# Experts 1 to 7: gathered rows transposed by DMA from two 16-bit planes, joined by ScalarE

## Chip, cores, metric

One core of a Trainium2 chip. The metric is the device time of one execution in microseconds (us). Engines are named as in the profile: PE is TensorE's matmul, PEld its weight load, DVE VectorE, ACT ScalarE, POOL GpSimd and SP SyncE, which here only issues DMAs. L12 is line 12 of the kernel before, unless said otherwise.

## The reference, cut to what matters

Three stages in float32: attention with a block-causal mask, a dense layer, and a mixture of eight experts of which each token takes two. N = 2304 tokens, D = 512, E = 8 experts, hidden size F = 1024.

```python
attn = softmax(mask(q @ k.T / sqrt(64)))           # 4 batches x 8 heads x 576 x 64
x = heads_joined(attn @ v)                          # 2304 x 512
h = maximum(maximum(x @ w1, x @ w2), x @ w3)        # 512 -> 768
x = h @ w_out                                       # 768 -> 512
logits = x @ w_gate + log1p(exp(x @ w_noise)) * noise
top2 = argpartition(-logits, 2, axis=1)[:, :2]
top2_w = softmax over the two logits
for e in range(8):
    for k in range(2):
        mask = top2[:, k] == e
        out[mask] += top2_w[mask, k, None] * (maximum(x[mask] @ W1[e], 0) @ W2[e])
```

## The kernel before, in words

Every float32 product is made as three PE products of halves: a value is split into `hi` (rounded to the matmul's type) and `lo = value - hi`, and hi·hi, lo·hi and hi·lo are summed in PSUM.

**Attention and the dense layer** run interleaved up to about 500 us. The dense layer works in nine units of 256 tokens. Its output for 128 tokens, `x2` (128 x 512 float32, a tile named "x2" of the pool `keep` with two buffers), goes to the DRAM array `x2d` through `store` (L847), one DMA of 256 KB on SP. The same two "x2" buffers are used by `init_out`, which fills the output with zeros. `route` then takes the two best experts of each token and writes token number and weight into lists by expert (`ids`, DRAM).

**The experts** come in eight rounds e, the one with most tokens after expert 0 first. The rows of one expert are taken in five chunks of 128, with capacities `CAPS[e]` of 640, 640, 624, 608, 600, 592, 584 and 576 rows.
- `gather(e)` (L1146): five indirect DMAs on POOL bring the rows by their numbers `ig` from `x2d` into tiles "xg", one token in a partition.
- `transposes(e)` (L1154): four PE transposes a chunk (L1167) bring the 512 columns into partitions, in PSUM; ACT copies the result to `xh` (L1169), and DVE subtracts to `xl` (L1170). There is one buffer each of `xh` and `xl`, so expert e + 1 can only write them when the first product of expert e has read them.
- `mm1(e, f)` (L1172): for eight column groups f, the first product: rows 0 to `CAPS[e]` - 256 and the last 256 apart, 12 products each (L1179 to L1181), then ReLU and its halves on ACT and DVE (L1183, L1184).
- `mm2(e, c)` (L1210): for a chunk c of rows, 24 products (L1227 to L1229) into 512 columns. For e > 0 the earlier output rows are gathered (`prev`, L1217, on POOL), DVE multiplies by the token's weight and adds, and an indirect DMA on POOL scatters the rows to the output (L1235).
- Weights (`load_expert`, L163): six pieces an expert, 768 KB (128 x 1536) or 512 KB (128 x 1024). Each is loaded on SP (L173, L178) into one of two buffers "rw", copied to the high half by ACT (L186) and subtracted to the low half by POOL (L187). A piece is fetched by `next(nw)` in the loop over the first product's f and in the second product.

Expert 0 begins while the last unit of the dense layer runs; its hidden values take the tiles of the dense layer and others as these come free. For this `free` (L1191) holds a list of names. Its last five entries are "hx", "x2", "hx", "x2", "hx": the tail parts of the hidden values for f = 4 and f = 6, rows 384 on, lie in the two "x2" buffers. They are read by the last two chunks of expert 0's second product.

The main loop at the kernel's end (printed below) sets the order: for expert e the first product with the next weights between, then `gather(e + 1)`, then the second product, with `transposes(e + 1)` behind its third chunk (behind the fourth chunk for e = 0). The program is scheduled by the framework from that order: each engine has its own instructions in a fixed order and waits on semaphores.

Of the kernel before, what the change touches and what calls it, by code (L numbers as in the profile page):

```python
# [7 lines left out]
F32 = mybir.dt.float32  # L8
# [4 lines left out]
U16 = mybir.dt.uint16  # L13
AF = mybir.ActivationFunctionType
# [3 lines left out]
B, H, S, D = 4, 8, 576, 64  # L18
DM, FF = 512, 768
NTOK = B * S  # L20
E, F2, CAP = 8, 1024, 640
# [4 lines left out]
CAPS = (640, 640, 624, 608, 600, 592, 584, 576)  # L26
# [3 lines left out]
CE = 3  # L30
# [94 lines left out]
def plain(ap):  # L125
    return ap.bitcast(F32)
# [3 lines left out]
def tile_attention_moe_moe(ctx, tc, qT, kT, v, w1, w2, w3, w_out, gates, noise, e1, e2, out):  # L130
    nc = tc.nc
# [3 lines left out]

    w1, w2, w3, w_out = (x.bitcast(I32) for x in (w1, w2, w3, w_out))
    x2d = nc.dram_tensor("x2d", [NTOK, DM], F32).ap()
    xld = nc.dram_tensor("xld", [4, 128, 2, UT], F32).ap()
    owd = nc.dram_tensor("owd", [E * NTOK, 1], F32).ap()
    ids = nc.dram_tensor("ids", [E * CAP, 2], F32).ap()  # L140
# [20 lines left out]
    XG, XGT = {}, {}  # L161
# [30 lines left out]
    keep = ph3.enter_context(tc.tile_pool(name="keep", bufs=1))  # L192
    moe = ph2.enter_context(tc.tile_pool(name="moe", bufs=1))
    att = ph1.enter_context(tc.tile_pool(name="att", bufs=1, side="right"))
# [17 lines left out]
    def new_set(q, kv, p, pt):  # L212
        nc.gpsimd.memset(p[:, 448:704].rearrange("p (a c) -> p a c", a=2)[:, :, 0:64], 0.0)
        SET.append((q, kv[:, 0:256], kv[:, 256:512].rearrange("p (r c) -> p r c", r=2), p,
                    pt.rearrange("p (r c) -> p r c", r=2)))

    new_set(*(att.tile([128, n], F32, name=x) for x, n in (("qe", 512), ("kve", 512), ("pe", 768), ("pte", 768))))
    LT = {x: n for x, n in (("Qh", 640), ("Ql", 640), ("Kh", S), ("Kl", S), ("V", 1280), ("Ph", 2560), ("Pl", 2560))}
    t = {x: att.tile([128, n], F32, name=x) for x, n in LT.items()}
    new_set(t["Qh"][:, :512], t["Kh"][:, :512], t["Ph"][:, :768], t["Ph"][:, 768:1536])  # L220
    new_set(t["Ql"][:, :512], t["Kl"][:, :512], t["Ph"][:, 1536:2304], t["Pl"][:, :768])
    new_set(t["V"][:, :512], t["V"][:, 512:1024], t["Pl"][:, 768:1536], t["Pl"][:, 1536:2304])

    nc.vector.tensor_scalar(ident, jp, 0.0, None, op0=OP.is_equal)
    nc.vector.tensor_scalar(before, jp, 0.0, None, op0=OP.is_gt)
# [20 lines left out]
    RAW, VV, QK, ST = {}, {}, {}, {}  # L246

    def at(j):
        late, b, g = JOBS[j]
        return b * H + 2 * g  # L250
# [27 lines left out]

    def load_values(j):
        n = LJ.index(j) % 2  # L280
        VV[j] = att.tile([128, 1280 if n else 640], F32, name=("rv", "V")[n])[:, :640].rearrange("p (r c) -> p r c", r=2)
        nc.sync.dma_start(VV[j], v[at(j):at(j) + 2].rearrange("h p c d -> p h (c d)"))

    def split_keys(j, low):
# [354 lines left out]
    def start():  # L639
# [141 lines left out]
        add("SP", 1.0, lambda: nc.sync.dma_start(noise_sb, noise.rearrange("(t p) e -> p t e", p=128)), [x, q8], 5.0, late=2.0, load=5.0)  # L781
        v8 = add("SP", 0.45, lambda: load_rest(8), [EV[7]], 4.0, late=2.0, load=0.5)
        add("SP", 0.45, lambda: load_values(first), [EV[6]], 4.0, late=2.0, load=0.8)
        add("POOL", 0.45, late_tails, [], 4.0)
        late_q = [add("POOL", 0.65, lambda n=n: late_queries(n), [ES[4 + n, 0], ES[4 + n, 1]], 3.0) for n in (0, 1)]
# [61 lines left out]
    def store(u, tt, x2):  # L847
        r0 = (u * 2 + tt) * 128
        nc.sync.dma_start(x2d[r0:r0 + 128, :], x2)

    def logits():
        return keep.tile([128, 2, 2 * E], F32, name="gl", bufs=2)
# [47 lines left out]
    rows = consts.tile([128, NU * 2, 2, 2], F32, name="rows")  # L900
# [147 lines left out]
    def late_after(j):  # L1048
        return next((x for x in LJ if x > j), NJ)
# [28 lines left out]
    for tt in range(2):  # L1078
        store(0, tt, C0[tt])
# [4 lines left out]
    RAW.pop(first)  # L1084
    load_job(late_after(first))
    load_values(late_after(first))
    scored(8)
    gap(8)
    for j in range(8, NJ):
        b, g = JOBS[j][1:]  # L1090
        T, SS = turn_steps(j), score_steps(j + 1)
        for n in range(max(len(T), len(SS))):
            if n < len(T):
                T[n]()
            if n < len(SS):
                SS[n]()
            gap(j)
        if j + 1 < NJ:
            scored(j + 1)
        pv(j)  # L1100
        if LATE[j]:
            n = late_after(j)
            if n < NJ:
                n = late_after(n)
                if n < NJ:
                    load_values(n)
        elif following(j):
            load_rest(following(j))
        gap(j)
        gap(j)  # L1110
        if all(x[:2] != JOBS[j][:2] for x in JOBS[j + 1:]):
            ready.add(2 * b + LATE[j])
        if 8 <= j < 8 + NU:
            init_out(j - 8)
# [7 lines left out]
    mw = ph1.enter_context(tc.tile_pool(name="mw", bufs=1, side="right"))  # L1122
# [3 lines left out]
    def bank2():  # L1126
        turn[0] ^= 1
        if turn[0]:
            return ps2.tile([128, 512], F32, name="b")
        return psT.tile([128, 512], F32, name="t", bufs=4)  # L1130
# [14 lines left out]

    def gather(e, c0=0, c1=NCH, rows=NTOK):  # L1146
        for c in range(c0, c1):
            x = mw.tile([128, DM], F32, name="xg", bufs=6)
            nc.gpsimd.indirect_dma_start(
                out=x, out_offset=None, in_=x2d[:rows],  # L1150
                in_offset=bass.IndirectOffsetOnAxis(ap=ig[:, e, c:c + 1], axis=0))
            XG[e, c] = x

    def transposes(e, c0=0, c1=NCH):  # L1154
        if c0 == 0:
            XGT[e] = [mw.tile([128, 4, CAP], F32R, name=n) for n in ("xh", "xl")]
        th, tl = XGT[e]
        for c in range(c0, c1):
            if e == 0 and c < CE and BT:
                ps = ps2.tile([128, 512], F32, name="b")  # L1160
            else:
                ps = bank2()
            ps = ps.rearrange("p (k t) -> p k t", k=4)
            n = min(128, CAPS[e] - 128 * c)
            ps = ps[:, :, :n]
            for kt in range(4):
                nc.tensor.transpose(ps[:, kt], XG[e, c][:n, kt * 128:(kt + 1) * 128], ident[:n, :n])  # L1167
            s = slice(c * 128, c * 128 + n)
            nc.scalar.activation(th[:, :, s], ps, AF.Copy)  # L1169
            nc.vector.tensor_sub(tl[:, :, s], ps, plain(th[:, :, s]))  # L1170

    def mm1(e, f, ht, parts=None, get=bank2):  # L1172
        parts = parts or ((0, CAPS[e] - 256), (CAPS[e] - 256, CAPS[e]))
        th, tl = XGT[e]
        for c0, c1 in parts:
            ps = get()
            p = ps[:, :c1 - c0]
            for kt in range(4):
                nc.tensor.matmul(p, wt1(e, 0, kt, f), th[:, kt, c0:c1], start=kt == 0, stop=False)  # L1179
                nc.tensor.matmul(p, wt1(e, 0, kt, f), tl[:, kt, c0:c1], start=False, stop=False)  # L1180
                nc.tensor.matmul(p, wt1(e, 1, kt, f), th[:, kt, c0:c1], start=False, stop=kt == 3)  # L1181
            hi, lo = (ht(t, c0, c1) for t in range(2))
            nc.scalar.activation(hi, p, AF.Relu)  # L1183
            nc.vector.scalar_tensor_tensor(lo, p, 0.0, plain(hi), op0=OP.max, op1=OP.subtract)  # L1184

    def hidden_tile(pool):
        t = pool.tile([128, 2, CAP], F32R, name="ht", bufs=8)
        return lambda s, c0, c1: t[:, s, c0:c1]
# [5 lines left out]
    def spare(shape):  # L1194
        pool, n, c = free.pop(0)
        return pool.tile(shape, F32R, name=n, bufs=c)
# [46 lines left out]
    def weights_of(e):  # L1243
        for m in range(2):
            yield from load_expert(e, m, rw)
# [88 lines left out]
    for e in range(E):  # L1334
        nw = weights_of(e + 1) if e + 1 < E else iter(())
        if e == 1:
            ph2.close()
            hid = ph2.enter_context(tc.tile_pool(name="hid", bufs=1))
        if e:
            HT = [hidden_tile(hid) for _ in range(8)]  # L1340
        for f in range(8):
            if e:
                mm1(e, f, HT[f])
            else:
                more[f].append(spare([128, 2, CAP - 128 * CE]))
                mm1(e, f, HT[f], ((128 * CE, CAP),))
            if f in (0, 1, 3, 6):
                next(nw, None)
        if e + 1 < E:
            gather(e + 1)  # L1350
        for c in range(0 if e else CE, NCH):
            mm2(e, c, HT)
            if c == (0 if e else CE):
                next(nw, None)
            if c == (2 if e else CE) and e + 1 < E:
                transposes(e + 1)
        for _ in nw:
            pass
    ph1.close()
# [98 lines left out]
```

## Time and profile before

| | |
|---|---|
| median of 3 runs | 985.82 us (985.78 to 988.04) |
| profiled execution | 986.13 us |
| its span, first to last instruction | 984.4 us |
| mean granted clock of TensorE | 0.998 of full speed |
| PE busy | 971.0 us, 99%, 6594 instructions |
| DVE busy | 431.2 us, 44% |
| ACT busy | 395.5 us, 40% |
| POOL busy | 392.6 us, 40% |
| DMA | 106.17 MB, 108 GB/s over the span |

The times of the text are those of the profiled execution, counted from the span's start. A busy share is the time in which an engine works on instructions, over the span; DMA issues on POOL count as POOL work of about 1 us each. Matmuls overlap: one shows a duration of 0.39 us and the next starts 0.23 us after it. The spacing of two starts tells what one costs.

### The profile page before, as it was taken

To read this page: it belongs to the slowest core of one execution; us is meant where nothing else is said; L and a number is where in the kernel's file an instruction comes from. 1 tells how busy PE (TensorE), PEld (TensorE's weight loads), DVE (VectorE), ACT (ScalarE), POOL (GpSimd) and SP (SyncE) were. 2 spreads that over 40 slices of the span, in tenths; PEclk is the share of its full clock that TensorE was granted. 3 is DMA by queue.
4 is the path that set the end of the run, shared out by engine and by line. 5 is a ranking of instruction groups with operands and counts; after the bars stand their busy time and mean duration, and the time that the engine had idled before them with its cause. 6 is when DMAs were issued, how large, how long until landed. Compare 5 with 4: busy or idle time off the path is not lost. (4 is left out here: it accounts for less than half of the span.)

```text
span 984.4 us, 17147 instructions
## 1 busy us (share of the span) xinstructions
PE 971.0 (99%) x6594; PEld 861.2 (87%) x6594; DVE 431.2 (44%) x1259; ACT 395.5 (40%) x938; POOL 392.6 (40%) x298
## 2 busy tenths in 40 slices
PE   9999999999999999999999999999999999999997
PEld 5856899999898998999999889898988979898895
DVE  7854657654677665632355322222222222221321
ACT  7587545544565555531134234142323323132210
POOL 3595121211213013120221577755836556564302
PEclk9999999999999999999999999999999999999999
DMA  9912414221211312212022546543535354452101
GB/s 322 340 29 71 134 47 155 54 90 31 62 55 36 92 36 68 63 30 85 22 81 82 173 160 196 180 151 108 184 108 162 109 155 146 126 170 77 52 14 57
DMA packets 72550, 106.17 MB, mean 108 GB/s; under 512 B 19196, under 2 KB 44796, under 8 KB 72464
## 3 DMA queue, kind: packets, MB, share of 16 engines
q1 hardware_dynamic: 61120, 75.93, 24.1%
q0 software_dynamic: 10224, 28.32, 8.8%
q8 instruction: 53, 0.87, 0.4%
q10 hardware_dynamic: 1120, 0.79, 0.3%
q14 instruction: 33, 0.27, 0.1%
HBM read 85.35 MB, written 20.53 MB: 108 GB/s over the span
## 5 line engine op out<-in xcount | busy, mean ns | idle before, releaser
L187 POOL TENSOR_TENSOR w<-rw,w 128x1536 fp32r<-128x1536 f32 (+1 forms) x42 | 131.7, 3137 | 71.7 <-ACT w L186 56.2
L827 POOL TENSOR_TENSOR hl<-hm,hh 128x512 fp32r<-128x512 f32 x21 | 27.7, 1317 | 173.3 <-ACT hh L826 173.2
L186 ACT ACTIVATE w<-rw 128x1536 fp32r<-128x1536 f32 (+1 forms) x42 | 56.5, 1345 | 89.2 <-issue 42.1
L1179 PE MATMUL b<-xh,w 128*128 128x384 f32 (+7 forms) x272 | 87.4, 322 | 0.7 <-DVE xB L1184 0.4
L1180 PE MATMUL b<-xl,w 128*128 128x384 f32 (+7 forms) x272 | 87.4, 321 | 0.3 <-DVE xl L1170 0.3
L1181 PE MATMUL b<-xh,w 128*128 128x384 f32 (+7 forms) x272 | 87.6, 322 | 0.0
L811 PE MATMUL t<-xA,w 128*128 128x256 f32 x288 | 83.1, 289 | 0.0
L812 PE MATMUL t<-xA,w 128*128 128x256 f32 x288 | 81.7, 284 | 0.0
L813 PE MATMUL t<-xA,w 128*128 128x256 f32 x288 | 81.5, 283 | 0.0
L1184 DVE SCALAR_TENSOR_TENSOR ht<-b,ht 128x384 fp32r<-128x384 f32 (+6 forms) x56 | 29.1, 520 | 94.3 <-ACT ht L1183 94.3
L1235 POOL DMA_INDIRECT out_rows<-y,isc x37 | 37.5, 1013 | 77.3 <-DVE y L1232 73.1
L1180 PE MATMUL t<-xl,w 128*128 128x256 f32 x240 | 67.3, 280 | 0.0
L1181 PE MATMUL t<-xh,w 128*128 128x256 f32 x240 | 67.3, 280 | 0.0
L1179 PE MATMUL t<-xh,w 128*128 128x256 f32 x240 | 67.3, 281 | 0.0
L1227 PE MATMUL b<-w,ht 128*128 128x512 f32 (+1 forms) x168 | 67.0, 399 | 0.0
L291 POOL TENSOR_TENSOR Kl<-rk,Kh 128x576 fp32r<-128x576 f32 x16 | 23.2, 1450 | 109.0 <-ACT Kh L288 109.0
L1229 PE MATMUL b<-w,ht 128*128 128x512 f32 (+1 forms) x168 | 66.4, 395 | 0.0
L1228 PE MATMUL b<-w,ht 128*128 128x512 f32 (+1 forms) x168 | 66.3, 394 | 0.0
L999 POOL DMA_INDIRECT ids<-rows,slots x36 | 35.9, 996 | 68.4 <-DVE slots L996 60.1
L811 PE MATMUL t<-xB,w 128*128 128x256 f32 x216 | 61.9, 287 | 0.0
L812 PE MATMUL t<-xB,w 128*128 128x256 f32 x216 | 61.3, 284 | 0.0
L813 PE MATMUL t<-xB,w 128*128 128x256 f32 x216 | 61.2, 283 | 0.0
(404 smaller groups left out, 2766.7 us busy)
## 6 DMA issues: line engine op xcount, KB each, us to landing
rw<-in_e SPq DMA_DIRECT2D x32, 768.0 KB, 4.6
w<-in_w SPq DMA_DIRECT2D x18, 512.0 KB, 7.8
rw<-in_e SPq DMA_DIRECT2D x16, 512.0 KB, 3.7
rk<-in_kT SPq DMA_DIRECT2D x16, 288.0 KB, 2.8
x2d<-x SPq DMA_DIRECT2D x18, 256.0 KB, 2.0
out_rows<-x SPq DMA_DIRECT2D x9, 512.0 KB, 3.0
w<-in_w_out SPq DMA_DIRECT2D x6, 512.0 KB, 10.1
rq<-in_qT SPq DMA_DIRECT2D x16, 160.0 KB, 2.3
```

Of the source, the lines that this page charges most:

```text
L186: nc.scalar.activation(t[:, 0, :c], r[:, :c], AF.Copy)
L187: nc.gpsimd.tensor_sub(t[:, 1, :c], r[:, :c], plain(t[:, 0, :c]))
L811: nc.tensor.matmul(ps[:, j], wh, x[:, 0], start=kt == 0, stop=False)
L812: nc.tensor.matmul(ps[:, j], wh, x[:, 1], start=False, stop=False)
L813: nc.tensor.matmul(ps[:, j], wl, x[:, 0], start=False, stop=kt == 3)
L1179: nc.tensor.matmul(p, wt1(e, 0, kt, f), th[:, kt, c0:c1], start=kt == 0, stop=False)
L1180: nc.tensor.matmul(p, wt1(e, 0, kt, f), tl[:, kt, c0:c1], start=False, stop=False)
L1181: nc.tensor.matmul(p, wt1(e, 1, kt, f), th[:, kt, c0:c1], start=False, stop=kt == 3)
L1227: nc.tensor.matmul(ps, a, wt2(e, 0, f), start=f == 0, stop=False)
L1228: nc.tensor.matmul(ps, a, wt2(e, 1, f), start=False, stop=False)
L1229: nc.tensor.matmul(ps, l, wt2(e, 0, f), start=False, stop=f == 7)
L1235: st = nc.gpsimd.indirect_dma_start(out=out, out_offset=bass.IndirectOffsetOnAxis(ap=at, axis=0), in_=y, in_offset=None, bounds_check=NTOK ...
```

## The change

Beside `x2d` there is a second DRAM array `x2p` of 16-bit words, 1024 a token: first the low halves of its 512 float32 words, then the high halves. `store` has POOL copy `x2` into such planes (tile "xp", one buffer) and stores them with a second DMA on SP. To make room, attention's tile "V" falls from 1280 to 768 words, some load buffers are cut out of it in smaller pieces, and "xg" has five buffers instead of six.

For experts 1 to 7 `gather` reads `x2p`. `transposes` then transposes a chunk of 128 x 1024 16-bit words by one DMA on SP into a tile "x2" (the same name and two buffers as above), as eight blocks of 128 x 128. ACT joins the two planes back into 32-bit words in the chunk's "xg" tile, ACT copies to `xh` as before, now from SBUF, and POOL, not DVE, subtracts to `xl`. Expert 0 is left as it was. `transposes(e + 1)` stands right behind `gather(e + 1)`, ahead of the second product of expert e.

```diff
+    x2p = nc.dram_tensor("x2p", [NTOK, 2 * DM], U16).ap()
...
-    LT = {x: n for x, n in (("Qh", 640), ("Ql", 640), ("Kh", S), ("Kl", S), ("V", 1280), ("Ph", 2560), ("Pl", 2560))}
+    LT = {x: n for x, n in (("Qh", 640), ("Ql", 640), ("Kh", S), ("Kl", S), ("V", 768), ("Ph", 2560), ("Pl", 2560))}
...
     def store(u, tt, x2):
         r0 = (u * 2 + tt) * 128
         nc.sync.dma_start(x2d[r0:r0 + 128, :], x2)
+        planes = keep.tile([128, 2, DM], U16, name="xp", bufs=1)
+        nc.gpsimd.tensor_copy(planes, x2.bitcast(U16).rearrange("p (d h) -> p h d", h=2))
+        nc.sync.dma_start(x2p[r0:r0 + 128].rearrange("r (h d) -> r h d", h=2), planes)
...
     def gather(e, c0=0, c1=NCH, rows=NTOK):
         for c in range(c0, c1):
-            x = mw.tile([128, DM], F32, name="xg", bufs=6)
+            x = mw.tile([128, DM], F32, name="xg", bufs=5)
+            if e:
+                x = x.bitcast(U16)
             nc.gpsimd.indirect_dma_start(
-                out=x, out_offset=None, in_=x2d[:rows],
+                out=x, out_offset=None, in_=x2p if e else x2d[:rows],
                 in_offset=bass.IndirectOffsetOnAxis(ap=ig[:, e, c:c + 1], axis=0))
             XG[e, c] = x
...
         th, tl = XGT[e]
         for c in range(c0, c1):
+            if e:
+                n = min(128, CAPS[e] - 128 * c)
+                s = slice(c * 128, c * 128 + n)
+                tp = keep.tile([128, DM], F32, name="x2", bufs=2).bitcast(U16).rearrange("p (k t) -> p k t", k=8)
+                nc.sync.dma_start_transpose(tp, XG[e, c])
+                x = XG[e, c].bitcast(F32).rearrange("p (k t) -> p k t", k=4)
+                nc.scalar.activation(x.rearrange("p k t -> p (k t)").bitcast(U16).rearrange("p (c h) -> p h c", h=2),
+                                     tp.rearrange("p (h k) t -> p h (k t)", h=2), AF.Copy)
+                nc.scalar.activation(th[:, :, s], x[:, :, :n], AF.Copy)
+                nc.gpsimd.tensor_sub(tl[:, :, s], x[:, :, :n], plain(th[:, :, s]))
+                continue
...
         if e + 1 < E:
             gather(e + 1)
+            transposes(e + 1)
         for c in range(0 if e else CE, NCH):
             mm2(e, c, HT)
             if c == (0 if e else CE):
                 next(nw, None)
-            if c == (2 if e else CE) and e + 1 < E:
-                transposes(e + 1)
```

How the instructions stand is shown at two places, both between expert 0 and expert 1. A name in brackets says what a row waits for: DMASW is a gather or scatter of POOL, DMAHW an earlier DMA of SP, and PE, DVE, Activation and Pool that engine.

SP before, weight loads only (L178 and L173, an ISA row sets an address from the expert's number):

```order
L178 DMA rw<-in_e 128x2x512 [waits DMAHW5_49,DMAHW3_49,Pool_49]
L173 ISA
L173 DMA rw<-in_e 128x4x384 [waits DMAHW6_49,DMAHW4_49,Pool_49]
L173 ISA
L173 DMA rw<-in_e 128x4x384 [waits DMAHW7_49,DMAHW5_49,Pool_49]
```

SP in the changed kernel, at the same loads (their lines are now L179 and L174, and x_7032 and the like are "x2" tiles):

```order
L179 DMA rw<-in_e 128x2x512 [waits DMAHW7_49,DMAHW5_49,Pool_49]
L1169 DMA_TRANSPOSE x_7032<-xg 128x8x128 [waits DMASW4_49,DMAHW0_49,DVE_49,PE_49]
L1169 DMA_TRANSPOSE x_7037<-xg 128x8x128 [waits DMASW5_49,DMAHW1_49,DVE_49,PE_49]
L174 ISA
L174 DMA rw<-in_e 128x4x384 [waits DMAHW6_49,Pool_49]
L1169 DMA_TRANSPOSE x_7042<-xg 128x8x128 [waits DMAHW0_49,DMASW6_49,Activation_49]
L1169 DMA_TRANSPOSE x_7047<-xg 128x8x128 [waits DMAHW1_49,DMASW7_49,Activation_49]
L174 ISA
L174 DMA rw<-in_e 128x4x384 [waits DMAHW7_49,Pool_49]
L1169 DMA_TRANSPOSE x_7052<-xg 128x8x128 [waits DMAHW3_49,DMASW0_49,Activation_49]
```

The five transposes of expert 1 stand between its last weight load and the first two loads for expert 2; the first two wait for PE, the others for ACT.

POOL before, from the last but one weight piece of expert 1 on (L187 weights, L1149 gathers for expert 2, L1235 scatter, L1217 earlier output rows):

```order
L187 TENSOR_TENSOR w<-rw,w 128x1536 [waits DMAHW4_49,Activation_49]
L1149 DMA xg<-x2d,ig 128x512 [waits DMASW7_49,PE_49]
L1149 DMA xg<-x2d,ig 128x512 [waits DMASW0_49,PE_49]
L187 TENSOR_TENSOR w<-rw,w 128x1024 [waits DMAHW5_49,Activation_49]
L1235 DMA out_rows<-y,isc 2304x512 [waits DMASW1_49,DVE_49]
L187 TENSOR_TENSOR w<-rw,w 128x1536 [waits DMAHW6_49,PE_49,Activation_49]
L1217 DMA prev_5388<-out_rows,isc 128x512 [waits DMASW5_49,DMASW2_49,DMASW1_49]
L1217 DMA prev_5387<-out_rows,isc 128x512 [waits DMASW3_49]
```

POOL in the changed kernel, from that expert's last weight piece on (lines 188, 1155, 1252 and 1234 now; L1174 is the subtraction to `xl`):

```order
L188 TENSOR_TENSOR w<-rw,w 128x1024 [waits DMAHW7_49,Activation_49]
L1252 DMA out_rows<-y,isc 2304x512 [waits DMASW3_49,DVE_49]
L1174 TENSOR_TENSOR xl<-xg,xh 128x4x128 [waits DMASW4_49,Activation_49]
L1174 TENSOR_TENSOR xl<-xg,xh 128x4x128 [waits DMASW5_49,Activation_49]
L1155 DMA xg<-x2p,ig 128x1024 [waits DMAHW0_49,Pool_49]
L188 TENSOR_TENSOR w<-rw,w 128x1536 [waits DMAHW2_49,Activation_49]
L1155 DMA xg<-x2p,ig 128x1024 [waits DMAHW1_49,Pool_49]
L1234 DMA prev_5424<-out_rows,isc 128x512 [waits DMASW3_49,DMASW6_49,DMASW2_49,DMASW1_49]
L1234 DMA prev_5423<-out_rows,isc 128x512 [waits DMASW7_49]
L1174 TENSOR_TENSOR xl<-xg,xh 128x4x128 [waits Activation_49] x2
L188 TENSOR_TENSOR w<-rw,w 128x1536 [waits DMAHW5_49,Activation_49]
L1174 TENSOR_TENSOR xl<-xg,xh 128x4x128 [waits DMASW0_49,Activation_49]
```

The five subtractions of expert 1 now stand in POOL's queue among weight pieces, gathers and reads of earlier rows. PE's order there has eight products of expert 1 with xh, then the products with the first 384 rows of xl, 36 up to the first that reads the last 256.

## Rows read from the trace of the kernel before

**Rows 1.** The page's first part: busy us, share of the span, instructions.
```profile
PE 971.0 (99%) x6594; PEld 861.2 (87%) x6594; DVE 431.2 (44%) x1259; ACT 395.5 (40%) x938; POOL 392.6 (40%) x298
```

**Rows 2.** Waits of PE from 500 us on: total us, times, longest.
```profile
PE b L1179 <- DVE xB L1184: 0.4, 1, 0.4
```

**Rows 3.** PE on the tile "xg": count, ns min/median/max, first and last start, shapes.
```profile
L1167 PE MATMUL t<-ident,xg x88: 221/272/273, 511.3 to 912.7; 128*128 128x128 f32 x64, 112*128 112x112 f32 x4, 96*128 96x96 f32 x4, 88*128 88x88 f32 x4
...
L1167 PE MATMUL b<-ident,xg x72: 270/273/273, 510.9 to 912.2; 128*128 128x128 f32 x72
```

**Rows 4.** Timeline of PE, expert 0 to 1: start us, us, instruction, [idle before <-releaser].
```profile
573.66 0.49 PE L1167 MATMUL b<-ident,xg 128*128 128x128 f32 x3
...
575.65 0.48 PE L1227 MATMUL t<-w,hl 128*128 128x512 f32 x1
...
579.01 0.40 PE L1229 MATMUL t<-w,x 128*128 128x512 f32 x1
...
580.40 0.39 PE L1229 MATMUL t<-w,x 128*128 128x512 f32 x1
...
581.74 0.62 PE L1179 MATMUL b<-xh,w 128*128 128x384 f32 x2 [0.24 <-ACT xh L1169]
```

**Rows 5.** Timeline of PE in expert 1's second product.
```profile
627.54 0.60 PE L1167 MATMUL t<-ident,xg 128*128 128x128 f32 x4
...
629.61 0.48 PE L1227 MATMUL b<-w,ht 128*128 128x512 f32 x1
```

**Rows 6.** The page's DMA issues: count, KB each, median us to landing.
```profile
rw<-in_e SPq DMA_DIRECT2D x32, 768.0 KB, 4.6
...
rw<-in_e SPq DMA_DIRECT2D x16, 512.0 KB, 3.7
...
x2d<-x SPq DMA_DIRECT2D x18, 256.0 KB, 2.0
...
w<-in_w_out SPq DMA_DIRECT2D x6, 512.0 KB, 10.1
...
xg<-x2d,ig POOLq DMA_INDIRECT x40, 3.6
```

**Rows 7.** Timeline of SP's queue, expert 0 to 1.
```profile
581.86 0.37 SPq L178 DMA_DIRECT2D rw<-in_e  x1
```

**Rows 8.** Timeline of POOL, expert 0 to 1.
```profile
578.32 3.51 POOL L187 TENSOR_TENSOR w<-rw,w 128x1536 fp32r<-128x1536 f32 x1 [4.97 <-ACT w L186]
...
583.25 0.95 POOL L1149 DMA_INDIRECT xg<-x2d,ig  x1 [0.30 <-issue]
```

**Rows 9.** ACT, expert 0 to 1, then its groups by form from 500 us on (busy us, mean ns).
```profile
585.66 1.06 ACT L186 ACTIVATE w<-rw 128x1024 fp32r<-128x1024 f32 x1 [3.00 <-DMA rw<-in_e]
...
L1169 ACT ACTIVATE xh<-b 128x512 fp32r<-128x512 f32 x18 | 10.8, 602 | 13.7 <-PE b L1167 13.7
```

**Rows 10.** Groups of POOL by form over the span: count, busy us, mean ns, idle before.
```profile
L187 POOL TENSOR_TENSOR w<-rw,w 128x1536 fp32r<-128x1536 f32 x28 | 98.1, 3506 | 67.7 <-ACT w L186 52.4 <-PE b L1181 13.1 <-PE t L1181 1.6
L1149 POOL DMA_INDIRECT xg<-x2d,ig x40 | 39.0, 976 | 33.5 <-PE t L1167 14.4 <-issue 8.4 <-DVE sq L1303 3.4
L1235 POOL DMA_INDIRECT out_rows<-y,isc x37 | 37.5, 1013 | 77.3 <-DVE y L1232 73.1 <-issue 2.2 <-DVE xl L1170 1.5
L1217 POOL DMA_INDIRECT prev<-out_rows,isc x35 | 35.9, 1027 | 12.6 <-issue 8.6 <-DMA out_rows<-y,isc 3.3 <-PE b L1181 0.3
...
L187 POOL TENSOR_TENSOR w<-rw,w 128x1024 fp32r<-128x1024 f32 x14 | 33.6, 2400 | 4.0 <-ACT w L186 3.8
L827 POOL TENSOR_TENSOR hl<-hm,hh 128x512 fp32r<-128x512 f32 x21 | 27.7, 1317 | 173.3 <-ACT hh L826 173.2
...
L557 POOL TENSOR_TENSOR w<-w 128x512 int32<-128x512 int32 x18 | 18.6, 1038 | 23.2 <-DVE w L544 20.6 <-ACT w L548 1.3 <-issue 0.5
```

**Rows 11.** Windows: length, busy us of PE, PEld, DVE, ACT, POOL (instructions), clock, DMA share, GB/s.
```profile
100.00:500.00 400.00, 396.06 (x3181) 368.02 (x3181) 228.56 (x769) 187.84 (x502) 80.29 (x67) 1.00 0.21 64
...
640.00:984.00 344.00, 337.76 (x1977) 299.04 (x1975) 82.28 (x152) 89.93 (x151) 175.71 (x111) 1.00 0.35 116
```

More of the change, by code (lines that the diff above doesn't have):

```diff
@@ L221, in tile_attention_moe_moe @@
     new_set(t["Ql"][:, :512], t["Kl"][:, :512], t["Ph"][:, 1536:2304], t["Pl"][:, :768])
-    new_set(t["V"][:, :512], t["V"][:, 512:1024], t["Pl"][:, 768:1536], t["Pl"][:, 1536:2304])
+    new_set(t["V"][:, :256], t["V"][:, 256:768], t["Pl"][:, 768:1536], t["Pl"][:, 1536:2304])
     nc.vector.tensor_scalar(ident, jp, 0.0, None, op0=OP.is_equal)
@@ L280, in load_values @@
         n = LJ.index(j) % 2
-        VV[j] = att.tile([128, 1280 if n else 640], F32, name=("rv", "V")[n])[:, :640].rearrange("p (r c) -> p r c", r=2)
+        VV[j] = att.tile([128, 768 if n else 640], F32, name=("rv", "V")[n])[:, :640].rearrange("p (r c) -> p r c", r=2)
         nc.sync.dma_start(VV[j], v[at(j):at(j) + 2].rearrange("h p c d -> p h (c d)"))
```

## Prediction

> **What bounds the kernel now.** Look first at the page's busy line: TensorE (PE) is busy for 99% of the span, the other engines for at most 44% [rows 1]. The list of PE's waits from 500 us to the end agrees: its longest is 0.4 us [rows 2]. So any instruction taken out of PE's stream is worth its full length, and any new wait of PE costs its full length, because nothing else is waiting in reserve. Next, the rows of the tile of gathered rows: 160 transposes in all, 88 into one PSUM name and 72 into the other [rows 3]. The timeline of two transitions between experts shows what twenty of them cost in place [rows 4, 5]. Last, POOL and SP around 582 us, where expert 0 ends and expert 1 begins [rows 7, 8], because the order of the changed kernel puts the new operations there.
>
> **Removed: 140 transposes.** Between the second and third chunk of expert 1's second product, PE spends 627.54 to 629.61 on twenty transposes, 2.07 us [rows 5]; at expert 0 it is 573.66 to 575.65, 1.99 us, with the first one ahead of that interval [rows 4]. I take 2.1 us each. Seven transitions give 14.7 us. Expert 0's own twenty stay. DVE loses 35 subtractions, and ACT's 35 copies read SBUF where they read PSUM (0.60 us [rows 9], left at that).
>
> **Added before the experts.** Each of 18 row blocks gets a POOL copy into two planes and one more 256 KB store; the store of that size that is there lands in 2.0 us [rows 6]. POOL shows no such copy. Its nearest rows are 1.04 us (512 words copied from one operand), 1.32 us (512 words of two operands) and 2.40 us (1024 words of two) [rows 10]; I take 2.4, since 1024 elements are moved with a stride. That is 18 x 2.4 = 43 us, in a stretch where POOL works 80 of 400 us [rows 11]. Idle POOL covers it. Without the cover a late copy would hold its "x2" buffer, and through it DVE and PE; that is a rival below.
>
> **Added per expert: five DMA transposes, five joins, five subtractions.** No DMA transpose is in the trace. The same 256 KB are moved by the block store in 2.0 us and by the gather in 3.6; the slowest transfer is a 512 KB load at 10.1 [rows 6]. I take 3.6, the gather being nearest (rows of 2 KB into 128 partitions), with 2.0 and 10.1 as ends. The join is an ACT pass over 1024 elements; ACT's row of that width takes 1.06 us [rows 9]; at the 0.60 of its copy the sum would hardly move, since POOL ends last below. The subtraction, 512 elements on POOL, goes by 1.32 [rows 10].
>
> From expert 2 on I count all this at nothing. The five gathers can go out once the subtractions of the expert before have read their buffers, most of an expert (344 / 6 = 57 us [rows 11]) before their rows are needed; only copy and subtraction wait for the single-buffered xh and xl, and these run under the second product, 120 matmuls at 0.232 us (six from 579.01 to 580.40 [rows 4]) or 28 us. POOL, busy 176 of 344 us there [rows 11], gets 5 x 1.32 x 6 = 40 us more. If the cover went, six transitions would pay part of 2.1 us back.
>
> **The new wait, expert 0 to expert 1.** The transposed tile has the name "x2" with two buffers. Until the end of expert 0, these hold two of its hidden tiles. So the first two DMA transposes wait for PE's last reads, 579.01 and 580.40 before [rows 4], 2.0 earlier now. In SP's order they also stand behind a weight load. That load went out at 581.86 [rows 7], released by the POOL subtraction from 578.32 of 3.51 us, thus ending at 581.83 [rows 8]. This does not move with PE. So the first transposes start at 582.2, and expert 1's first product, which began at 581.74 [rows 4] and could begin at 579.7, must wait. With 3.6 a transpose and 1.06 a join, and two buffers, the third transpose waits for the first join, and the fifth for the third:
> - ACT and DMA: landed 585.8; ACT's weight copy (585.66, 1.06 [rows 9]) goes first; join 587.8; third transpose 591.4, join 592.5; fifth 596.1, join 597.2; copy to xh 597.8.
> - POOL works in order: the weight subtraction of 3.5 (581.83 to 585.3), a scatter of 1.0, from 586.7 one of 2.4, a scatter (590.1), two xl subtractions (592.7), a gather (594), 3.5 of weights (597.5), a gather, two reads of previous rows (601.2), the third and fourth xl (603.8), 3.5 of weights, the fifth xl (608.6). All durations from [rows 8, 10], with 0.3 between DMA issues.
>
> PE's order there has eight xh products first, then 36 with xl on the first 384 rows, which need the third xl (602.5), then those on the last 256, which need the fifth. The 36 take 36 x 0.175 = 6.3 us, an estimate from the 0.232 of 512 columns (384 of 512). So PE restarts in earnest at 602.5 and meets the fifth xl at 608.8; less 1.2 us for the eight products already done, expert 1 starts effectively at 601.3, not 581.74: +19.6. In it the lost 2.0 of the first transition is already contained. The six other transitions give 6 x 2.1 = 12.6. **Sum: +7.0.** The profiled execution took 986.13, 0.3 above the median of 985.82, so 993.1 against the profile, 993 against the median.
>
> The granted clock is 1.00 in every window shown [rows 11], the higher of the two levels; PE is never idle for long here, so no row shows what an idle PE does to it. [...]
>
> **Rivals.**
> - *Half the wait* (about 988.6, no change). If POOL takes the subtractions before the weights' share, ACT and DMA decide: xh complete at 597.8, less 0.7 for four products done, 597.1; +15.4 - 12.6 = +2.8. For it: POOL has idle time. Against it: its order has the weights first.
> - *Faster* (about 983). Transposes at 2.0 and POOL not in the way: 584.2, 585.3, 587.3, 588.3, 590.3, 591.4, xh at 592.0; +9.6 - 12.6 = -3.0. With no wait at all it would be the full 14.7: 971. Against it: the wait on the "x2" buffers does not depend on a price.
> - *Dear transposes* (about 1032). At 10.1 each, xh is complete at 616.3, +34 - 12.6 = +21. Also SP stands in each expert for three rounds of transpose and join, 3 x 11.2 = 33.5 us, and behind it wait six weight loads of 4.6 and 3.7 us [rows 6], 25.8 in series; 59.3 against PE's 344 / 6 - 2.1 = 55.2 [rows 11], six times 4.1, +25. Sum +46. It decides from some 8.7 us a transpose, where the two are equal. For it: the tile has eight 128 x 128 blocks, and the transposition is in pieces of 2 bytes. [...]
> - *Copies in the way* (995 to 1010). If the plane copy takes far over 2.4 us, the next block's "x2" waits, and PE with it: 0.5 to 1 us in each of 18 blocks, +9 to +18, on top of a start that costs what I forecast or less. Against it: 80 of 400 us busy [rows 11].
> - That the change doesn't do what it says can be set aside: in the order of its PE stream 20 transposes are left.
>
> **How the numbers follow.** 0.3%, or 3 us, is about what a measurement of this kernel can tell from no change. Forecast 0.50 (its own range 989 to 1003: subtractions of 1.0 to 2.4, the clock), dear transposes 0.18, copies in the way 0.07: slower 0.75. Half the wait 0.14: same. Faster 0.11. The range 982 to 1032 goes from the faster rival to the dear end of the rows and leaves out some 0.13: full hiding below, a transpose beyond 10.1 us above.
>
> **What would show it.** Right: no transposes at 627; PE idle for 15 to 22 us after 579, waiting for POOL's xl; a DMA transpose of 3 to 5 us; no other wait over 1 us. Wrong: waits at each transition for POOL, ACT or the weights (dear transposes), waits before 500 us (copies), or PE going on at 580 without a stop.

## The result, and the profile after

The changed kernel takes 996.84 us (median of 4 runs, 994.25 to 998.28) against 985.80 of before: ratio 1.0104, 95% interval 1.0078 to 1.013. It is slower by about 1%. The profiled execution took 997.2 us, its span is 995.4. Where did 11 us come from, when PE has 140 transposes less to do?

The page's first part of the changed kernel shows it at once: PE is busy 960.1 us, 10.9 less than before [rows 1], and its share is 96%, not 99%.

```profile
PE 960.1 (96%) x6454; PEld 850.0 (85%) x6454; DVE 415.1 (42%) x1224; ACT 437.2 (44%) x973; POOL 453.1 (46%) x351
```

PE's waits from 500 us to the end (who waited for whom, us in total, times, longest), where before the longest was 0.4 [rows 2]:

```profile
PE t L1196 <- ACT xh L1173: 14.0, 1, 14.0
PE b L1196 <- ACT xh L1173: 3.3, 1, 3.3
PE t L1196 <- DVE ht L1201: 0.8, 1, 0.8
PE t L1197 <- POOL xl L1174: 0.7, 1, 0.7
```

Three of the four are one event, the start of expert 1's first product, 18.0 us together. PE's timeline there (start us, us, instruction, [idle before <-releaser]):

```profile
582.21 0.40 PE L1246 MATMUL b<-w,hx 128*128 128x512 f32 x1
596.61 1.65 PE L1196 MATMUL t<-xh,w 128*128 128x384 f32 x4 [14.00 <-ACT xh L1173]
601.55 1.22 PE L1196 MATMUL b<-xh,w 128*128 128x256 f32 x4 [3.29 <-ACT xh L1173]
603.42 0.69 PE L1197 MATMUL t<-xl,w 128*128 128x384 f32 x1 [0.65 <-POOL xl L1174]
603.91 0.52 PE L1198 MATMUL t<-xh,w 128*128 128x384 f32 x1
604.23 0.52 PE L1196 MATMUL t<-xh,w 128*128 128x384 f32 x1
...
608.61 0.34 PE L1196 MATMUL t<-xh,w 128*128 128x384 f32 x1
608.78 0.34 PE L1197 MATMUL t<-xl,w 128*128 128x384 f32 x1
```

Two things are to be read here. PE stands still, with two short bursts, from 582.6 to 603.4. And up to 608.4 its products of 384 columns start 0.32 us apart, later 0.17. The windows tell why (length, busy us of PE, PEld, DVE, ACT, POOL, granted clock, DMA share, GB/s):

```profile
560.00:582.00 22.00, 22.00 (x143) 19.92 (x143) 4.52 (x10) 9.34 (x13) 17.25 (x9) 1.00 0.59 208
582.00:596.00 14.00, 0.61 (x3) 0.17 (x1) 0.75 (x1) 8.92 (x10) 12.76 (x9) 0.59 0.91 227
596.00:609.00 13.00, 8.45 (x27) 7.65 (x28) 0.11 (x1) 7.59 (x9) 12.20 (x8) 0.52 0.80 206
609.00:640.00 31.00, 31.00 (x198) 29.64 (x197) 8.35 (x17) 15.95 (x26) 14.76 (x11) 1.00 0.43 122
```

After the idle stretch the granted clock is at a lower level: in windows of 0.2 us it is 1.00 up to 584.4, 0.50 from 584.6 to 608.4 and 1.00 again from 608.6 on. The first eight products are slow as well (1.65 and 1.22 us for four), but they end before the next wait does. What counts is the 16 after 603.4, at 0.32 instead of 0.173 us: 2.4 us.

What PE waited for: SP's queue, ACT and POOL in the same stretch, in three pieces.

```profile
582.90 3.37 SPq L1169 DMA_TRANSPOSE x<-xg  x2
...
588.90 3.13 SPq L1169 DMA_TRANSPOSE x<-xg  x2
...
594.91 4.79 SPq L1169 DMA_TRANSPOSE x<-xg  x2
```

```profile
586.48 1.06 ACT L187 ACTIVATE w<-rw 128x1024 fp32r<-128x1024 f32 x1 [4.39 <-DMA rw<-in_e]
587.52 1.35 ACT L1171 ACTIVATE xg<-x 128x1024 uint16<-128x1024 uint16 x1
...
593.54 2.55 ACT L1171 ACTIVATE xg<-x 128x1024 uint16<-128x1024 uint16 x2 [0.18 <-DMA x<-xg]
...
597.50 1.48 ACT L187 ACTIVATE w<-rw 128x1536 fp32r<-128x1536 f32 x1 [0.42 <-DMA rw<-in_e]
599.50 1.34 ACT L1171 ACTIVATE xg<-x 128x1024 uint16<-128x1024 uint16 x1 [0.51 <-DMA x<-xg]
600.87 0.63 ACT L1173 ACTIVATE xh<-xg 128x512 fp32r<-128x512 f32 x1
```

```profile
594.81 3.47 POOL L188 TENSOR_TENSOR w<-rw,w 128x1536 fp32r<-128x1536 f32 x1
...
602.09 2.50 POOL L1174 TENSOR_TENSOR xl<-xg,xh 128x512 fp32r<-128x512 f32 x2
...
607.99 1.29 POOL L1174 TENSOR_TENSOR xl<-xg,xh 128x512 fp32r<-128x512 f32 x1
```

The first transpose goes out at 582.90. PE's last product that reads an "x2" tile had started at 581.52, with 0.39 us; the weight load that stands ahead in SP's queue went out later, at 582.36, so by the trace it is this load that ended last, as the prediction had it. The third goes out at 588.90, when the first join has given its buffer back, and the fifth at 594.91, after the third join. ACT waits for the fifth until 599.50, so a transpose with its landing takes 4.6 us here (594.91 to 599.50). Over the whole kernel, 26 joins waited for their transpose; they began 3.5 to 12.2 us after it was issued, with a median of 4.6. The third xh is there when PE starts at 596.61, but POOL, in order, has a weight piece, a gather and two reads of earlier rows before the third xl, which it starts at 602.09.

The gain is there too: expert 1's second product runs on PE from 632.96 to 661.12, 28.2 us. Before, it ran from 610.75 to 641.04, 30.3 us, with the twenty transposes [rows 5] in it.

Last, PE was already 3.0 us late before the experts: matched by line and occurrence, its instructions from 140 to 520 us start 2.9 to 3.1 us later than before. Two waits are new, one that ends at 103.8 us and one that ends at 114.2 (PE's list of the stretch from 95 to 140 us):

```profile
PE s L314 <- DVE st L396: 2.0, 1, 2.0
PE a L315 <- DVE Ql L301: 1.9, 1, 1.9
```

The account of the profiled execution: expert 1's first product ends at 633.1 us, before at 610.9, +22.2; six transitions, 6 x 2.1 = -12.6; the first products of experts 3 and 6, where PE waits for ReLUs, are 1.0 and 0.6 us longer than before, +1.6. That is +11.2, and 997.2 - 986.13 is 11.1. The early 3.0 us don't stand in it: PE comes later to a wait whose end hangs on SP's weight load (582.36 against 581.86 before [rows 7]), so in this kernel the wait has swallowed most of them.

### The profile page after: what moved, and what is told of

Same layout as the page of the kernel before. It is cut to its first block, busy times and chain, and to the rows that moved or that the text cites. A ratio compares the mean times of both kernels' runs of the same rounds, so it can differ in the third digit from the quotient of the medians.

```text
span 995.4 us, 17074 instructions
## 1 busy us (share of the span) xinstructions
PE 960.1 (96%) x6454; PEld 850.0 (85%) x6454; DVE 415.1 (42%) x1224; ACT 437.2 (44%) x973; POOL 453.1 (46%) x351
## 5 line engine op out<-in xcount | busy, mean ns | idle before, releaser
L1171 ACT ACTIVATE xg<-x 128x1024 uint16<-128x1024 uint16 x35 | 47.7, 1367 | 117.2 <-DMA x<-xg 108.1
L187 ACT ACTIVATE w<-rw 128x1536 fp32r<-128x1536 f32 (+1 forms) x42 | 56.2, 1338 | 73.1 <-DMA rw<-in_e 52.6
L1196 PE MATMUL t<-xh,w 128*128 128x256 f32 (+4 forms) x240 | 73.6, 309 | 14.8 <-ACT xh L1173 14.0
L1196 PE MATMUL b<-xh,w 128*128 128x256 f32 (+4 forms) x272 | 82.5, 306 | 4.0 <-ACT xh L1173 3.3
L1198 PE MATMUL b<-xh,w 128*128 128x256 f32 (+4 forms) x272 | 82.2, 303 | 0.0
L1197 PE MATMUL b<-xl,w 128*128 128x256 f32 (+4 forms) x272 | 82.1, 302 | 0.0
L1197 PE MATMUL t<-xl,w 128*128 128x256 f32 (+4 forms) x240 | 73.8, 307 | 0.7 <-POOL xl L1174 0.7
L1198 PE MATMUL t<-xh,w 128*128 128x256 f32 (+4 forms) x240 | 73.5, 306 | 0.0
L1196 PEld LDWEIGHTS t<-xh,w 128*128 128x128 f32 x240 | 46.2, 193 | 15.7 <-ACT xh L1173 14.4
L1201 DVE SCALAR_TENSOR_TENSOR ht<-t,ht 128x256 fp32r<-128x256 f32 (+4 forms) x56 | 26.6, 475 | 77.4 <-ACT ht L1200 77.4
L852 POOL COPY xp<-x 128x1024 uint16<-128x1024 uint16 x18 | 19.5, 1082 | 85.5 <-DMA x2p<-xp 30.3
L321 ACT ACTIVATE p<-s,st 128x320 f32<-128x320 f32 (+1 forms) x64 | 38.8, 606 | 41.6 <-DVE st L320 40.9
L1244 PE MATMUL t<-w,ht 128*128 128x512 f32 (+3 forms) x144 | 57.0, 396 | 0.0
```

Source lines behind the costliest of these rows:

```text
L187: nc.scalar.activation(t[:, 0, :c], r[:, :c], AF.Copy)
L321: nc.scalar.activation(dst, src, AF.Exp, bias=st[:, 0, c:c + 1], scale=1.0, accum_out=st[:, 1, c:c + 1])
L1171: nc.scalar.activation(x.rearrange("p k t -> p (k t)").bitcast(U16).rearrange("p (c h) -> p h c", h=2), tp.rearrange("p (h k) t -> p h (k ...
L1244: nc.tensor.matmul(ps, a, wt2(e, 0, f), start=f == 0, stop=False)
```

## The experiments

The theory after the result had three parts: the wait at expert 1 comes from the two "x2" buffers that expert 0 still holds; the early 3 us come from the plane copies; the rest is the gain. Rivals: POOL's queue, the price of a DMA transpose wherever it stands, or the clock.

**Planes only.** Nothing reads the planes; all experts gather and transpose as before.

```diff
-                out=x, out_offset=None, in_=x2p if e else x2d[:rows],
+                out=x, out_offset=None, in_=x2d[:rows],
...
-            if e:
+            if e > 7:
                 n = min(128, CAPS[e] - 128 * c)
```

> The planes are made and stored, but no one reads them: all experts gather from x2d and transpose on TensorE in the old order. In the changed kernel's trace PE is 3.0 us late from 140 us on. If the plane copies hold the x2 buffers there, this run is 3.0 us above before, 988.8. Rival: the 3.0 us are chance or come from the experts' side: 985.8. If the copies cost more than the trace showed (rival of the prediction): 995 or more.

Measured: 988.09 us, ratio 1.0026 (1.0017 to 1.0036), so +2.7 us. The planes, with the smaller tile "V" and five "xg" buffers that make room for them, cost that much; POOL's copy itself is cheap (1.08 us, below).

**Expert 1 back on TensorE.**

```diff
-                out=x, out_offset=None, in_=x2p if e else x2d[:rows],
+                out=x, out_offset=None, in_=x2p if e > 1 else x2d[:rows],
...
-            transposes(e + 1)
+            if e:
+                transposes(e + 1)
...
+            if c == CE and e == 0:
+                transposes(1)
```

> Expert 1 alone goes back to TensorE transposes (gathered from x2d); experts 2 to 7 keep the DMA transposes. If the wait between expert 0 and 1 comes from the x2 buffers that hold expert 0's hidden values, it is gone, and no new one comes at expert 1 to 2: 985.8 + 3.0 - 6 x 2.1 + 1.6 of small waits = 977.8. Rival: the first DMA transposes are late wherever they stand (POOL's queue, SP's queue, their price): then the wait moves to expert 1 to 2 and the time stays at 990 or more.

Measured: 981.65 us (977.0 to 988.78 in 10 runs), ratio 0.9963 (0.9937 to 0.9988). The long wait is gone and doesn't move to expert 2, so it belongs to the DMA transposes at this one place and not to their price wherever they stand. Whether the "x2" buffers make it, this run can't tell, as it takes away everything that is special to expert 1; the next one can. But 3.9 us of the expected gain are missing and the runs are far apart. PE's list from 560 us on shows a wait that stood in no list so long:

```profile
PE b L1196 <- DVE ht L1201: 2.4, 1, 2.4
PE t L1196 <- DVE ht L1201: 2.4, 1, 2.4
```

Behind it is ACT, here around the first of the two (PE's wait ends at 613.32):

```profile
611.24 1.34 ACT L1171 ACTIVATE xg<-x 128x1024 uint16<-128x1024 uint16 x1 [1.92 <-DMA x<-xg]
612.46 0.35 ACT L1200 ACTIVATE ht<-t 128x256 fp32r<-128x256 f32 x1
```

The schedule has put joins among expert 1's ReLUs. ACT works in order and stood 1.92 us at this join until its transpose landed; the ReLU behind it came at 612.46, PSUM was not emptied, and PE stopped for 2.4 us.

**A tile of its own for the transposed rows.**

```diff
-                tp = keep.tile([128, DM], F32, name="x2", bufs=2)...
+                tp = (mw.tile([128, DM], F32, name="tp") if c % 2 else keep.tile([128, 2, DM], U16, name="xp", bufs=1)...)
...
-        y = mw.tile([128, DM], F32, name="y", bufs=2)[:n]
+        y = mw.tile([128, DM], F32, name="y", bufs=1)[:n]
```

> The transposed tile leaves the name x2: even chunks use the plane tile xp, free since the dense layer ended, odd chunks one tile of their own (room from y with one buffer instead of two). If the x2 buffers make the wait, expert 1's first transposes go out some 15 us earlier, at about 566, and PE's wait falls from 18 us to 8 or less: 996.8 - 10 to 14 = 983 to 987. Rival, the chain of ACT, POOL and SP's loads sets it: PE still waits 14 us or more, 993 or above.

Measured: 994.6 us (989.02 to 998.91), ratio 1.0078 (1.0055 to 1.0101). The total missed, the mechanism did not. SP's queue has the first transposes, now ahead of the weight loads that they stood behind, 20 us earlier than the changed kernel's 582.90:

```profile
563.24 1.37 SPq L1169 DMA_TRANSPOSE xp<-xg  x1
```

PE goes from expert 0 to expert 1 without a stop (0.7 us for xl). So the "x2" buffers made the long wait. PE then loses the time elsewhere, 8.6 us for `y`, which I had cut to one buffer, and 8.4 for the ReLUs as above (this profile is of the slowest of the seven runs; own tiles with two buffers for `y` were not run). The longest rows:

```profile
PE t L1196 <- DVE y L1249: 5.7, 4, 3.5
PE t L1196 <- DVE ht L1201: 4.5, 1, 4.5
```

**Subtraction to xl back on VectorE.**

```diff
-                nc.gpsimd.tensor_sub(tl[:, :, s], x[:, :, :n], plain(th[:, :, s]))
+                nc.vector.tensor_sub(tl[:, :, s], x[:, :, :n], plain(th[:, :, s]))
```

> The subtraction to xl goes back from POOL to DVE, reading SBUF; all else as in the changed kernel. The prediction had POOL's queue as what ends last at expert 1: then PE starts 4 us earlier, 992.5. The changed kernel's trace says DMA and ACT end last (14.0 and 3.3 us of wait for xh, 0.65 for xl): then about 0.7 us is gained, 996.

Measured: 992.07 us, ratio 1.0061 (1.0041 to 1.008): 4.8 us less than the changed kernel, as POOL's rival had it. PE's timeline shows how:

```profile
598.11 1.65 PE L1196 MATMUL t<-xh,w 128*128 128x384 f32 x4 [14.82 <-ACT xh L1173]
599.56 0.52 PE L1197 MATMUL t<-xl,w 128*128 128x384 f32 x1
```

The first xl is there with the third xh, so PE's order no longer puts the products with the fifth chunk's xh ahead, and the 3.3 us wait is gone. The long wait for xh stays. So both were true: DMA and ACT end last at the first product, POOL's place in the queue sets what comes behind it.

**Clock kept up.** 56 products whose sums no one reads fill PE's idle time.

```diff
+        if e == 0:
+            for _ in range(2):
+                ps = bank2()
+                for _ in range(28):
+                    nc.tensor.matmul(ps, EW[1, 0, 0][:, 0, :128], EW[1, 0, 0][:, 0, :512], start=True, stop=True)
```

> The changed kernel with 56 products of 512 columns whose sums no one reads (56 x 0.233 = 13.0 us) between expert 0's last product and expert 1's first, where PE was idle for 14.0 us. If the slow spacing behind that wait (0.32 us for 384 columns instead of 0.173, until 608.4) comes from the granted clock, which fell after the idle time, the spacing stays at 0.17 there, the mean clock from 560 to 640 us stays at 1.00 instead of 0.85, and 3.9 us are saved: about 993. Rival, data or transfers make the products slow: no change, 996.8, same spacing.

Measured: 998.04 us, ratio 1.0112 (1.0095 to 1.013), nothing saved. The windows and the timeline of this kernel:

```profile
582.00:596.00 14.00, 13.30 (x59) 10.65 (x57) 0.75 (x1) 8.68 (x9) 12.67 (x9) 1.00 0.85 213
596.00:604.00 8.00, 2.31 (x9) 1.70 (x9) 0.00 (x0) 5.01 (x6) 7.20 (x6) 0.74 0.90 247
604.00:611.00 7.00, 7.00 (x25) 7.00 (x26) 0.56 (x1) 3.31 (x4) 6.69 (x4) 0.57 0.66 161
```

```profile
597.10 0.97 PE L1196 MATMUL t<-xh,w 128*128 128x384 f32 x4 [1.79 <-ACT xh L1173]
601.87 1.22 PE L1196 MATMUL b<-xh,w 128*128 128x256 f32 x4 [3.81 <-ACT xh L1173]
```

With PE busy for 13.30 of the 14.00 us the clock stays at 1.00, and the first four products take 0.97 us, not 1.65. So the slow spacing is the clock's, not the data's. But after the gaps of 1.8 and 3.8 us it is down again (0.57 from 604 to 611), and 18 products come at 0.32. The fill kept the clock up where PE waits anyway, not where it counts (and ReLUs cost 3.5 us in this profile, which is of the slowest of the four runs); the wait itself has to go.

**Each transpose twice**, on the kernel with expert 1 on TensorE.

```diff
                 nc.sync.dma_start_transpose(tp, XG[e, c])
+                nc.sync.dma_start_transpose(tp, XG[e, c])
```

> As the run with expert 1 on TensorE (981.7), but each of the 30 DMA transposes is issued twice into the same tile, one after the other: the price goes from some 4.6 to some 9.2 us a tile. By the prediction's rival of dear transposes, which decides from 8.7 us, the time rises by 6 x 3 us or more, 995 to 1000; if the price is hidden as it stands in experts 2 to 7 and has room to spare, it stays within 3 us of 981.7.

Measured: 999.42 us, ratio 1.0114 (1.0068 to 1.016), 17.8 above the 981.65 it is compared with. From 560 us on PE's list now has 14.0 us of waits for hidden values, spread over the experts. The joins that waited now began 5.8 to 22.2 us after the first issue, with a median of 10.2. So a price of about double is not hidden where the joins stand among the ReLUs. Whether 4.6 us is, the next run shows.

**Joins held behind the ReLUs**, expert 1 on TensorE. DVE first writes one word of the expert's last hidden value into the first two transposed tiles, so the transposes can't go before it.

```diff
+                if c < 2:
+                    nc.vector.tensor_copy(tp[0:1, 0:1], plain(after)[0:1, 0:1])
...
-                transposes(e + 1)
+                transposes(e + 1, after=HT[7](0, 0, 128))
```

> As the run with expert 1 on TensorE, and in experts 2 to 7 the DMA transposes wait for the last ReLU of the expert before (DVE first writes one word of it into the transposed tile), so that ACT's joins stand behind the ReLUs of that expert and not among them. If ACT, in order, waiting at a join for a transpose, held back the ReLUs and so PE (2.4 us twice in that run's profile, and its spread from 977 to 989), the waits for ht go and the time is 985.4 + 2.7 - 12.6 = 975.5, with a narrow spread. Rival: the spread has another cause, 981 with the same spread; or 20 us of chain don't fit under the second product: waits for xh or xl at every expert, over 985.

Measured: 975.64 us (974.85 to 978.06), ratio 0.9891 (0.9875 to 0.9908). The transposes, at a median of 4.7 us, are hidden: all of PE's waits from 560 us on are now one row:

```profile
PE b L1200 <- DVE xl L1190: 0.2, 1, 0.2
```

**The early 2.7 us** took two runs. First the zeros of the output two jobs later, on planes only:

```diff
-        if 8 <= j < 8 + NU:
-            init_out(j - 8)
+        if 10 <= j < 10 + NU:
+            init_out(j - 10)
```

> As the run with planes only, and the zeros of the output are written two jobs later (they use the x2 buffers too, and DVE writes them). If the 2.7 us of that run are DVE waiting for the first two x2 tiles, which POOL has still to copy at 96 and 100 us, they are gone: 985.4. Rival, the copies or the second store cost by themselves: 988.

Measured: 987.85, ratio 1.0025 (1.0015 to 1.0035). No effect, and no evidence either: SP sends the first zeros at 105.3 us, as it did at 105.6 in the changed kernel, so the edit did not move them. Next the zeros got a tile of their own, 128 x 256, written once:

```diff
-        z = keep.tile([128, DM], F32, name="x2", bufs=2)
-        nc.vector.memset(z, 0.0)
...
+        for h in range(2):
+            nc.sync.dma_start(out[256 * j:256 * j + 256, 256 * h:256 * h + 256].rearrange("(t p) d -> p t d", p=128),
+                              zero[:, None, :].to_broadcast([128, 2, 256]))
```

> As the run with planes only, but the zeros of the output come from a small tile of their own, written once, so that they take no x2 buffer and DVE does not write zeros among its softmax work. If DVE standing at a zero fill that waits for an x2 buffer is what the planes cost (2.7 us in that run), the time is 985.4 again. Rival, the 18 copies and stores cost by themselves: 988.

Measured: 985.22, ratio 0.9995 (0.9985 to 1.0006). The loss is gone with all 18 copies and stores, and the smaller "V", in place. So it hangs on the zero fills: on the "x2" buffers that they take, or on their place among DVE's work. How they delay PE is shown only in part. The changed kernel's DVE:

```profile
103.45 0.17 DVE L396 RECIPROCAL st<-s 128x2 f32<-128x2 f32 x1
...
105.13 0.48 DVE L925 MEMSET x<- 128x512 f32 x1
...
109.00 0.48 DVE L925 MEMSET x<- 128x512 f32 x1 [1.29 <-DMA out_rows<-x]
```

PE's second new wait (1.9 us, for `Ql`) ends at 114.2. On DVE the zero fill at 109.00, which waits for an "x2" buffer, and two more at 111.80 and 112.75 stand ahead of that `Ql`; with zeros apart this wait is gone. The first (2.0 us, for the reciprocal of a softmax) ends with the reciprocal at 103.45, before any zero fill, and most of it is still there with zeros apart:

```profile
PE s L314 <- DVE st L396: 1.5, 1, 1.5
```

Why this wait is new stays open. Zeros apart in the kernel before, without planes, were not run, so they may gain something by themselves.

**All together:** expert 1 on TensorE, joins held, zeros apart.

> Expert 1 on TensorE, joins held behind the ReLUs, and the small tile of zeros: all costs found are out, the gain of six transitions stays. 985.6 - 12.6 = 973; if the zeros are not the cause of the 2.7 us, 975.6 as in the run with the joins held.

Measured: 972.71 us (971.19 to 973.44), ratio 0.9874 (0.9857 to 0.989). This beats both kernels, by 12.8 us the one before. No wait of PE from 500 us on is above 0.4 us.

## Why the prediction was right

It said 993 us, slower, by a new wait between expert 0 and 1 that costs more than the other transitions give back. Measured 996.84, 3.8 more. Between the profiled executions it is 4.1 (997.2 against 993.1), by the account above 2.6 at that wait and 1.6 at later ReLUs.

- *Transitions.* 2.1 us each: 30.3 to 28.2 us in expert 1's second product; the version with joins held gains six of them. Right.
- *The new wait.* Forecast: expert 1's first product 19.6 us late, measured 22.2. The step, POOL's queue sets it, held: the third xl came at 603.4 (forecast 602.5), the fifth at 609.3 (608.6). The prices on the other chain were too low: a transpose took 4.6 us, not 3.6, a join 1.37, not 1.06, and three weight copies of ACT, not one, stood among the joins. So the fifth xh came at 601.5, not 597.8, but still 1.9 ahead of the third xl. In PE's list only 0.7 us stand to POOL's xl, where the prediction's sign had the whole wait; the other 17.3 stand to the eight xh products that PE's order has in front, and these do not set the end. The run with xl on VectorE shows POOL's part: 4.8 us, against 4.2 by the prediction's sums (19.6 less 15.4). What I had left out of the sum is the clock: PE took 8.7 us for the 36 products, not 6.3, and reached the last 256 rows at 612.1 instead of 608.8 (0.9 of it POOL, 2.4 the clock); the fifth xl decided nothing. The short waits with which expert 1 began before (0.24 us for xh [rows 4], one more for xl) are no longer there, which gives some of it back: 2.6 remain.
- *The clock.* While PE stood still the granted clock went from 1.00 to 0.50 (at 584.6), and it was at 1.00 again at 608.6, 5.2 us after PE had gone on without a pause: 0.59 and 0.52 in the two windows from 582 to 609, then 1.00. In the forecast's own range, 989 to 1003, "the clock" is a term whose size no row or run shows; the runs showed 2.4 us on the path in its place.
- *"Idle POOL covers" the plane copies: the step that failed.* The copy took 1.08 us, under half of my 2.4 [rows 10], yet the planes cost 2.7 us, though POOL was free. I had looked at its time, not at who else uses the "x2" buffers that the copy reads: the loss is gone once the zero fills leave them, and DVE. The copy's group among POOL's, busy us, mean ns, and what it waited for:

```profile
L852 POOL COPY xp<-x 128x1024 uint16<-128x1024 uint16 x18 | 19.5, 1082 | 85.5 <-DMA x2p<-xp 30.3 <-ACT x L844 27.8 <-issue 27.4
```

  The rival "copies in the way" was near, a loss before 500 us, perhaps by way of the "x2" buffers; but it is one delay of 3 us near the start (PE's lag stays at 2.9 to 3.1 us from 140 to 520), not 18 small ones, and with a cheap copy. That it hardly shows in the total is luck: the wait at expert 1 swallowed most of it.
- *"At nothing" from expert 2 on* was nearly right in the changed kernel (1.6 us), but by luck of the schedule: the cover I named is PE's second product, and I did not see that the joins would be put under the first one, among ReLUs. With expert 1 on TensorE the same placing cost 6.0 us (981.65 against 975.64 with the joins held).
- *Dear transposes.* A tile of eight blocks takes 4.6 us in the median and 12.2 at most: 1.0 above the 3.6 of the forecast, under half of the rival's 10.1. The store of the same bytes takes 2.0 and the gather 3.6 [rows 6], so the DMA transpose was the dearest of the three, though neither of the others goes from SBUF to SBUF. The point from which the rival decides, some 8.7 us, stays untested: the run with double transposes is 17.8 us slower, but its waits are for hidden values, behind joins on ACT, not for weight loads behind transposes on SP, as the rival had it.

## What to carry to other kernels

Removing work from the bounding engine pays in full only where its replacement is ready in time (here six transitions gave 2.1 us each, and the one where it was not cost 22.2): at each transition ask which buffer the first new transfer needs and who still reads it. An operation that waits for a DMA must not stand, on an in-order engine, ahead of the work that empties PSUM; a false dependency that holds it back was worth 6 us here (981.65 to 975.64). Look at who else uses a new operation's buffers, not only at an engine's free time: a cheap copy (1.08 us) on an idle engine cost 2.7 us, and they came back when the zero fills left the buffers that it reads, and DVE.

## Not expected

- A pause of PE of 1.8 and 3.8 us, with four products between, was enough for the granted clock to fall again in the run with the fill (1.00 from 582 to 596 us, 0.57 from 604 to 611).
- The runs of three kernels that have joins among ReLUs lie 10 to 12 us apart (977.0 to 988.8; 989.0 to 998.9; 991.9 to 1001.5 with double transposes); with the joins held back it is 3 us (974.9 to 978.1, four runs). But it is no rule: the changed kernel's runs lie 4 us apart (994.3 to 998.3), and with xl on VectorE 1.6. Why was not tried, and no run shows it.
